# Batch 1's loads and attention pulled into the first layer, global rows on the ACT queue, one score run per pair, in a fused windowed-attention and two-layer kernel

## Chip, cores, metric

One core of one Trainium2 chip. The metric is the device time of one execution in microseconds (us), taken as the median of several executions. Engines are named as in the profile: PE (matmul), PEld (weight load), DVE, ACT, POOL, SP. The granted clock is the share of the full PE clock that the profile shows as granted; a slow PE clock is called cold, a full one warm.

## The reference

Per batch and head there are 512 local rows with a window of 32 to each side, and 32 global rows that see everything and are seen by everything. The attention output (8 batches x 544 rows x 512 columns) goes through two layers with a hard-swish between them.

```python
s_g   = scale * q_g @ concat(k_g, k_l).T;  out_g = softmax(s_g) @ concat(v_g, v_l)
s_ll  = where(|i - j| <= 32, scale * q_l @ k_l.T, -1e9)
out_l = softmax(concat(scale * q_l @ k_g.T, s_ll)) @ concat(v_g, v_l)
x = concat(out_g, out_l).transpose(0, 2, 1, 3).reshape(8 * 544, 512)
h = x @ w_in                       # 512 -> 2048
out = (h * clip(h + 3, 0, 6) / 6) @ w_out   # 2048 -> 512
```

## The kernel before

Attention works on "pairs" (two heads of one batch, `p = 4*b + m`, 32 of them). Layers work on "units": `u1(c)` is one of 16 units of layer 1 (four 512-column matmuls into one PSUM bank, a ReLU on ACT, an eviction `gt` on DVE), `u2(t, c4)` one of 16 units of layer 2 (four matmuls). `M(n)` emits the next n units of the batch before, between pieces of attention. There are seven general PSUM banks. `pin` fixes the order of the instructions traced so far to the program's order; what is not pinned, the build's scheduler may move. Each engine has its own list of instructions; in the trace of the kernel after, all 502 counted instructions of DVE start in the order in which the compiled program lists them (compared by source line).

A pair needs: casts of k, q, v (DVE or POOL), transposes (`emit_T` on PE, `emit_TD` by DMA for batches from 2 on), scores (`emit_S`, two chunks), exponentials on ACT, masks on DVE, `emit_AV`, and for the global rows `emit_SG` and `emit_PG`. `emit_G` casts and transposes the global keys or queries of several batches. `kglob` and `vglob` copy global rows beside a batch's local ones.

```python
# loads, all on SP, through 13 staging tiles
for i in range(NC):  load_w("in", i)
for i in range(NC):
    load_w("out", i)
    if i == 3:
        load_g(1, 4, "kg"); load_g(0, 4, "qg")      # 7 global-row loads, 64 KB each
for p in range(NM, 2 * NM + 1):                     # batch 1 and the next pair
    load(p)
...
# after the attention of batch 0: layer 1 of batch 0 with nothing between its units
for c in range(HEAD, NC):
    u1(c)
for i in range(NC):
    cast_w("out", i, nc.gpsimd)
emit_G(1, 4, "kg"); emit_G(0, 4, "qg")
fill_v(1, nc.vector); fill_vg(1, nc.gpsimd)
kglob(1, nc.gpsimd); vglob(1, nc.gpsimd)
for p in range(NM, 2 * NM):
    cast(p, "k", nc.vector); cast(p, "qv", nc.gpsimd); vshift(p, nc.gpsimd)
M(3)                                                # layer 2 of batch 0 begins
pin(*ALL)
emit_T(4)                                           # attention of batch 1
...
# the loop, one pair a turn; n = how many layer units go where
M(n[0]); emit_S(p + 1, 0)
M(n[1]); emit_S(p + 1, 1); emit_SG(p + 1)
M(n[2]); emit_AV(p); emit_PG(p)
M(n[3]); emit_X(p)
```

The softmax here doesn't subtract the row's maximum and nothing guards it: scores larger than these inputs give would overflow.

Of the kernel before, what the change touches and what calls it, by code (L numbers as in the profile page):

```python
# [14 lines left out]
def kernel(  # L15
# [94 lines left out]
    def stage():  # L110
        return wrk.tile([P, 512], FP32, tag="stg", name="stg", bufs=NSTG)

    def load(p, what="kqv"):
        b, m = divmod(p, NM)
        s = st.setdefault(p, {})
        for c in what:
            src = {"k": k_l, "q": q_l, "v": v_l}[c]
            t = stage()
            if c != "v" and b < NRUN:
                nc.sync.dma_start(out=t.rearrange("p (h x) -> p h x", h=2),  # L120
                                  in_=src[b, 2 * m:2 * m + 2].rearrange("h (p j) d -> p h (j d)", j=NT))
            else:
                nc.sync.dma_start(out=t.rearrange("p (h kb d) -> p (h kb) d", h=2, kb=NT),
                                  in_=src[b, 2 * m:2 * m + 2].rearrange("h (kb p) d -> p (h kb) d", p=P))
            s[c + "f"] = t.rearrange("p (h kb d) -> p kb h d", h=2, kb=NT)
# [12 lines left out]
    def vshift(p, eng, n=1):  # L138
        b, m = divmod(p, NM)
        hs = slice(2 * m, 2 * m + 2 * n)  # L140
        eng.tensor_copy(out=vbs[b % NV][0:D, :, hs, 0:D], in_=vts[b % NV][D:P, :, hs, 0:D])  # L141
# [12 lines left out]
    def load_w(kind, i):  # L154
        t = stage()
        if kind == "in":
            qd, m = divmod(i, NM)
            nc.sync.dma_start(out=t, in_=moe_w_in[m * P:(m + 1) * P, qd * 512:(qd + 1) * 512])
        else:
            nc.sync.dma_start(out=t, in_=moe_w_out[i * P:(i + 1) * P, :])  # L160
        w_st[kind, i] = t

    def cast_w(kind, i, eng):
        if kind == "in":
            qd, m = divmod(i, NM)
            o = w_in_t[m][:, qd * 512:(qd + 1) * 512]
        else:
            o = w_out_t[i // 4][:, i % 4]
        eng.tensor_copy(out=o, in_=w_st[kind, i])

    gst = {}

    def load_g(b0, b1, nm):
        src = {"kg": k_g, "qg": q_g}[nm]
        t = stage()
        for b in range(b0, b1):
            i = b - b0
            nc.sync.dma_start(out=t[i * Sg:(i + 1) * Sg].rearrange("s (h d) -> s h d", h=H),
                              in_=src[b].rearrange("h s d -> s h d"))
        gst[b0, nm] = t  # L180

# [53 lines left out]
    def wrap_q(p):  # L235
        qT = st[p]["qT"]
        nc.gpsimd.tensor_copy(out=qT[:, 0:W], in_=qT[:, Sl:Sl + W])  # L237

    def emit_S(p, ch, pe_mask=False):
        s = st[p]  # L240
        qT, kT = s["qT"], s["kT"]
        if ch == 0:
            s["E"] = wrk.tile([P, 2, 2, Sl], FP16, tag="E", name="E", bufs=3)
        E = s["E"]
        pss = [ps_tile(f"psS{e}") for e in range(2)]
        if pe_mask:
            for e in range(2):
                nc.tensor.matmul(out=pss[e], lhsT=ident, rhs=mneg[:, ch], start=True, stop=False,
                                 skip_group_check=True)
        for w in range(NT):  # L250
            c0 = w * KW if ch == 0 else ((w - 1) % NT) * KW + D
            for e in range(2):
                r = slice(e * D, (e + 1) * D)
                nc.tensor.matmul(out=pss[e][:, w * P:(w + 1) * P], lhsT=kT[r, c0:c0 + P],  # L254
                                 rhs=qT[r, w * P:(w + 1) * P], start=not pe_mask, stop=True,
                                 skip_group_check=True)
        for e in range(2):
            nc.scalar.activation(out=E[:, ch, e], in_=pss[e], func=EXP, scale=qk_scale)  # L258
        for e in range(0 if pe_mask else 2):
            nc.vector.tensor_tensor(out=E[:, ch, e], in0=E[:, ch, e],  # L260
                                    in1=mk[:, ch].rearrange("p w c -> p (w c)"), op=mult)
# [19 lines left out]
    def emit_AV(p):  # L281
        b, m = divmod(p, NM)
        E = st[p]["E"]
        vt, vb = vts[b % NV], vbs[b % NV]
        xn = wrk.tile([P, NT, P], FP16, tag="xn", name="xn", bufs=3)
        st[p]["xn"] = xn
        for w2 in range(NT // 2):
            po = ps_tile("pav").rearrange("p (w c) -> p w c", w=2)
            for i in range(2):
                w = 2 * w2 + i  # L290
                for e in range(2):
                    h = 2 * m + e
                    o = po[:, i, e * DV:e * DV + D + 1]
                    nc.tensor.matmul(out=o, lhsT=E[:, 0, e, w * P:(w + 1) * P],  # L294
                                     rhs=vt[:, w, h, 0:D + 1], start=True, stop=False,
                                     skip_group_check=True)
                    nc.tensor.matmul(out=o, lhsT=E[:, 1, e, w * P:(w + 1) * P],  # L297
                                     rhs=vb[:, (w - 1) % NT, h, 0:D + 1], start=False, stop=True,
                                     skip_group_check=True)
            pv = po[:, :, 0:2 * DV].rearrange("p w (e c) -> p w e c", e=2)  # L300
            rc = wrk.tile([P, 2, 2, 1], FP32, tag="rc", name="rc", bufs=4)
            nc.vector.reciprocal(out=rc, in_=pv[:, :, :, D:D + 1])  # L302
            nc.vector.tensor_tensor(  # L303
                out=xn[:, 2 * w2:2 * w2 + 2].rearrange("p w (e d) -> p w e d", e=2),
                in0=pv[:, :, :, 0:D], in1=rc.to_broadcast([P, 2, 2, D]), op=mult)
# [103 lines left out]
        load(p, "kqv")  # L409
    for i in range(NC):  # L410
        load_w("in", i)
    for i in range(NC):
        load_w("out", i)
        if i == 3:
            load_g(1, 4, "kg")
            load_g(0, 4, "qg")
    for p in range(NM, 2 * NM + 1):
        load(p)

    make_identity(nc, ident)  # L420
    load_vg(0)
# [16 lines left out]
    def fill_v(i, eng):  # L438
        eng.memset(vbs[i], 0.0)
        eng.memset(vbs[i][0:P - W, :, :, D:D + 1], 1.0)  # L440
        eng.memset(vts[i][:, :, :, D:D + 1], 1.0)
# [6 lines left out]
    def fill_vg(i, eng):  # L448
        eng.memset(vgs[i], 0.0)
        eng.memset(vgs[i][rg, :, D:P], 1.0)  # L450
# [38 lines left out]
    emit_S(3, 0, True)  # L489
    emit_X(1)  # L490
    emit_S(3, 1, True)
    emit_AV(2)
    HEAD = 3
    for c in range(HEAD):
# [10 lines left out]
    for t in Egs:  # L505
        nc.vector.memset(t[:, NT], 0.0)
    nc.vector.tensor_scalar(out=mk.rearrange("p c w q -> p c (w q)"), in0=mneg, scalar1=-1.0,
                            scalar2=1.0, op0=is_ge, op1=mult)
    for c in range(HEAD, NC):
        u1(c)  # L510
    for i in range(NC):
        cast_w("out", i, nc.gpsimd)
    emit_G(1, 4, "kg")
    emit_G(0, 4, "qg")
    fill_v(1, nc.vector)
    fill_vg(1, nc.gpsimd)
    kglob(1, nc.gpsimd)
    vglob(1, nc.gpsimd)
    for p in range(NM, 2 * NM):
        cast(p, "k", nc.vector)  # L520
        cast(p, "qv", nc.gpsimd)
        vshift(p, nc.gpsimd)
    M(3)
    pin(*ALL)
    emit_T(4)
    emit_SG(0)
    emit_SG(1)
    M(1)
    emit_SG(2)
    emit_SG(3)  # L530
    emit_S(4, 0)
    M(1)
    for p in range(NM):
        emit_PG(p)
    emit_T(5)
    emit_S(4, 1)
    ones_v(1)
    emit_SG(4)
    emit_XG(0)
    for b in range(2, B):  # L540
        load_vg(b)

    for p in range(NM, NPAIR):
        b, m = divmod(p, NM)
        if p + 5 < NPAIR:
            load(p + 5)
        if 2 * NM <= p + 2 < NPAIR:
            wrap_q(p + 2)
        if p + 4 < NPAIR:
            if m == 0:  # L550
                vglob(b + 1, nc.gpsimd)
            cast(p + 4, "kqv", nc.gpsimd)
            vshift(p + 4, nc.gpsimd)
        if m == 1 and b + 1 < B:
            kglob(b + 1, nc.gpsimd)
        if p == 5:
            load_g(4, B, "kg")
            load_g(4, B, "qg")
        if p == 10:
            emit_G(4, B, "kg")  # L560
            emit_G(4, B, "qg")
        n = (1, 1, 0, 0) if b == 1 else (1, 2, 2, 3)
        if 2 * NM <= p + 3 < NPAIR:
            emit_TD(p + 3)
        if p + 2 < 2 * NM:
            emit_T(p + 2)
        M(n[0])
        if p + 1 < NPAIR:
            emit_S(p + 1, 0)
        M(n[1])  # L570
        if p + 1 < NPAIR:
            emit_S(p + 1, 1)
            emit_SG(p + 1)
        M(n[2])
        emit_AV(p)
        emit_PG(p)
        M(n[3])
        emit_X(p)
        if m == NM - 1:
            emit_XG(b)  # L580
            units += moe_units(lambda mm, b=b: xts[b][mm], Sl, local_dests(b))
        pin(*QUEUES)
    M(len(units))
    units += moe_units(
        lambda mm: xg[:, mm].rearrange("p b s -> p (b s)"), B * Sg,
# [33 lines left out]
```

## Time and profile before

| | before |
|---|---|
| median time | 339.18 us (3 runs, 339.06 to 340.31) |
| span of the profiled run | 337.4 us |
| PE busy | 93% |
| mean granted clock | 0.967 |
| layer 1 of batch 1 starts (chain) | 83.28 us |

The table by windows of the kernel before follows. After the stretch and its length come the busy time of each engine with its instruction count, the granted TensorE clock, the DMA share and GB/s.

```profile
core 0: us, PE busy (x) PEld busy (x) DVE busy (x) ACT busy (x) POOL busy (x), PEclk, DMA share, GB/s
0.00:20.00 20.00, 12.60 (x154) 6.82 (x156) 13.79 (x40) 14.78 (x26) 15.38 (x33) 1.00 0.99 280
20.00:36.80 16.80, 16.08 (x112) 7.80 (x108) 13.57 (x32) 10.60 (x17) 10.47 (x17) 1.00 0.96 294
36.80:83.30 46.50, 36.76 (x412) 20.62 (x412) 30.58 (x73) 22.15 (x54) 35.79 (x59) 0.78 1.12 230
83.30:299.00 215.70, 215.70 (x1925) 107.75 (x1924) 148.26 (x323) 136.81 (x272) 70.98 (x132) 1.00 0.71 140
...
```

From 83.3 to 299 us PE never stands still and its clock is full, so only fewer PE cycles can help there. Between 36.8 and 83.3 us PE stands for 9.7 us, and its clock averages 0.78. The waits of PE in that part (engine, line, what it waited for, then us in total, times, longest):

```profile
PE psTq L213 <- POOL qn L136: 2.6, 1, 2.6
PE psS L254 <- DVE qT L221: 2.3, 2, 2.0
PE psGT L188 <- DVE kgn L185: 1.8, 1, 1.8
PE pg L317 <- ACT Eg L272: 1.5, 1, 1.5
PE psGT L188 <- DVE qgn L185: 1.0, 1, 1.0
...
```

POOL's time line (start, us, engine, line, operation, output and input, count) just before that cast:

```profile
45.77 2.28 POOL L145 COPY vb<-vg 32x512 f16<-32x512 f16 x4
47.99 0.81 POOL L147 COPY vgs<-vg 32x512 f16<-32x512 f16 x1
48.87 0.61 POOL L136 CAST qn<-stg 128x512 f16<-128x512 f32 x1
```

By the landing events packed with the trace, the query that this cast reads had landed at 44.60 us. POOL came to it only after its own w_out casts, fills and global-row copies.

The chain of work that ended last (start, us, what) shows what the scores cost PE in steady state:

```profile
124.85 1.83 PE psH L360 x8
126.68 0.33 PE psS L254 x8
127.01 0.25 PE psSG L271 x5
127.26 1.73 PE psH L360 x8
...
```

Eight layer matmuls take 1.73 us, but 1.83 us right after a score run. A score run of eight matmuls takes 0.33 us.

### The profile page before, as it was taken

How to read it: one execution, taken by the hardware profiler on the slowest of the kernel's cores; microseconds unless marked ns; L12 is line 12 of the kernel's file. 1: busy time of each engine (PE TensorE's matmuls, PEld its weight loads, DVE VectorE, ACT ScalarE, POOL GpSimd, SP SyncE). 2: the span in 40 equal slices, each digit the busy share in tenths (PEclk: the TensorE clock that was granted, in tenths of full speed). 3: DMA queues.
4: the chain of work that ended last, by engine and by line, in shares of the span. 5: the costliest groups of instructions: out<-in, count | busy, mean ns of one | idle time of the engine just before them, and what ended most of it. 6: DMA issues, size and time to landing. Idle time of an engine off the chain costs nothing.

```text
span 337.4 us, 7429 instructions
## 1 busy us (share of the span) xinstructions
PE 314.6 (93%) x2780; PEld 161.0 (48%) x2780; DVE 220.8 (65%) x494; ACT 198.2 (59%) x393; POOL 132.6 (39%) x240
## 2 busy tenths in 40 slices
PE   1989669959999999999999999999999999999994
PEld 0554236535454445454444554454445445444571
DVE  4868846875895588547866787468744882483160
ACT  8648308655883488447844785468645971382260
POOL 5985799863753362319313725182230000000000
PEclk9999876987999999999999999999999999999999
DMA  8999999979995977788799897897943002101202
GB/s 210 318 377 226 338 292 246 175 176 183 198 202 113 213 165 139 151 185 179 140 145 199 174 143 140 176 216 142 137 114 96 18 16 80 62 0 33 84 11 62
DMA packets 139747, 52.92 MB, mean 157 GB/s; under 512 B 127168, under 2 KB 131264, under 8 KB 139712
## 3 DMA queue, kind: packets, MB, share of 16 engines
q1 hardware_dynamic: 137536, 52.19, 71.5%
q0 software_dynamic: 2176, 0.26, 1.2%
q8 instruction: 22, 0.36, 0.5%
q14 instruction: 13, 0.11, 0.1%
HBM read 35.13 MB, written 8.91 MB: 131 GB/s over the span
## 4 chain that ended last, share of the span: by engine, by line
PE 83%; DMA 7%; ACT 3%; DVE 3%; POOL 1%; issue 1%; SPq 1%; DVEq 0%; POOLq 0%
PE po L376 36%; PE psH L360 31%; PE psS L254 5%; DMA stg<-in_moe_w_out_dram 3%; DMA stg<-in_moe_w_in_dram 3%; PE psSG L271 2%; PE pav L297 2%; PE pav L294 2%; PE pg L317 2%; ACT vt L445 1%; DVE E L260 1%; PE psX L333 1%; POOL vb L145 1%; SPq L160 1%; ACT E L258 1%
## 5 line engine op out<-in xcount | busy, mean ns | idle before, releaser
L376 PE MATMUL po<-wout,gt 128*128 128x512 f16 x544 | 131.6, 390 | 0.0
L360 PE MATMUL psH<-xt,win 128*128 128x512 f16 x512 | 117.3, 379 | 0.5 <-DVE xt L337 0.5
L367 DVE SCALAR_TENSOR_TENSOR gt<-t,psH 128x512 f16<-128x512 f32 (+1 forms) x144 | 90.6, 654 | 23.2 <-ACT t L365 21.5
L365 ACT ACTIVATE t<-psH,half_col 128x512 f32<-128x512 f32 (+1 forms) x144 | 92.1, 664 | 21.9 <-PE psH L360 19.1
L258 ACT ACTIVATE E<-psS 128x512 f16<-128x512 f32 x128 | 69.1, 598 | 52.3 <-PE psS L254 52.2
L360 PEld LDWEIGHTS <-win 128*128 128x128 f16 x576 | 53.5, 98 | 53.9 <-issue 0.6
L376 PEld LDWEIGHTS <-gt 128*128 128x128 f16 x544 | 50.9, 100 | 55.9 <-issue 5.4
L260 DVE TENSOR_TENSOR E<-E,mk 128x512 f16<-128x512 f16 x112 | 55.5, 515 | 33.1 <-ACT E L258 32.1
L237 POOL COPY qT<-qT 128x32 f16<-128x32 f16 x24 | 5.0, 209 | 109.9 <-DMA qT<-qn 103.3
L380 ACT COPY ot<-po 128x512 f32<-128x512 f32 x17 | 10.0, 586 | 38.5 <-PE po L376 38.5
L254 PEld LDWEIGHTS <-kT 64*128 64x128 f16 x512 | 15.1, 96 | 28.9 <-issue 25.4
L254 PE MATMUL psS<-qT,kT 64*128 64x128 f16 x512 | 26.2, 225 | 2.3 <-DVE qT L221 2.3
L303 DVE TENSOR_TENSOR xn<-pav,rc 128x256 f16<-128x256 f32 x64 | 26.5, 423 | 1.4
L380 DVE COPY ot<-po 128x512 f32<-128x512 f32 x17 | 11.8, 692 | 21.3 <-PE po L376 21.3
L141 POOL COPY vb<-vt 64x512 f16<-64x512 f16 x32 | 20.7, 647 | 2.1
L136 POOL CAST vt<-stg 128x512 f16<-128x512 f32 x32 | 20.7, 648 | 1.9 <-DMA stg<-in_v_l_dram 1.9
L136 POOL CAST qn<-stg 128x512 f16<-128x512 f32 x32 | 20.2, 630 | 1.6 <-DMA stg<-in_q_l_dram 1.3
L297 PE MATMUL pav<-vb,E 128*128 128x65 f16 x256 | 20.3, 195 | 0.0
L294 PE MATMUL pav<-vt,E 128*128 128x65 f16 x256 | 20.3, 194 | 0.0
L294 PEld LDWEIGHTS <-E 128*128 128x128 f16 x256 | 18.0, 99 | 3.1
L302 DVE RECIPROCAL rc<-pav 128x4 f32<-128x4 f32 x64 | 10.6, 174 | 12.4 <-PE pav L297 12.4
L297 PEld LDWEIGHTS <-E 128*128 128x128 f16 x256 | 17.2, 98 | 2.8
(73 smaller groups left out, 239.6 us busy)
## 6 DMA issues: line engine op xcount, KB each, us to landing
stg<-in_k_l_dram SPq DMA_DIRECT2D x32, 256.0 KB, 3.5
stg<-in_q_l_dram SPq DMA_DIRECT2D x32, 256.0 KB, 4.1
stg<-in_v_l_dram SPq DMA_DIRECT2D x32, 256.0 KB, 4.5
out_dram<-ot SPq DMA_DIRECT2D x24, 256.0 KB, 2.3
stg<-in_moe_w_in_dram SPq DMA_DIRECT2D x16, 256.0 KB, 5.9
stg<-in_moe_w_out_dram SPq DMA_DIRECT2D x16, 256.0 KB, 5.2
out_dram<-ot SPq DMA_DIRECT2D x8, 192.0 KB, 2.2
out_dram<-ot SPq DMA_DIRECT2D x16, 64.0 KB, 1.9
```

The costliest lines, as they stand in the source:

```text
L136: eng.tensor_copy(out=o, in_=s[c + "f"])
L254: nc.tensor.matmul(out=pss[e][:, w * P:(w + 1) * P], lhsT=kT[r, c0:c0 + P], rhs=qT[r, w * P:(w + 1) * P], start=not pe_mask, stop=True, sk ...
L258: nc.scalar.activation(out=E[:, ch, e], in_=pss[e], func=EXP, scale=qk_scale)
L260: nc.vector.tensor_tensor(out=E[:, ch, e], in0=E[:, ch, e], in1=mk[:, ch].rearrange("p w c -> p (w c)"), op=mult)
L294: nc.tensor.matmul(out=o, lhsT=E[:, 0, e, w * P:(w + 1) * P], rhs=vt[:, w, h, 0:D + 1], start=True, stop=False, skip_group_check=True)
L297: nc.tensor.matmul(out=o, lhsT=E[:, 1, e, w * P:(w + 1) * P], rhs=vb[:, (w - 1) % NT, h, 0:D + 1], start=False, stop=True, skip_group_chec ...
L303: nc.vector.tensor_tensor(out=xn[:, 2 * w2:2 * w2 + 2].rearrange("p w (e d) -> p w e d", e=2), in0=pv[:, :, :, 0:D], in1=rc.to_broadcast([ ...
L360: nc.tensor.matmul(out=ps[:, 0:n], lhsT=w_in_t[m][:, c * P:(c + 1) * P], rhs=rhs(m), start=(m == 0), stop=(m == NM - 1), skip_group_check= ...
L365: nc.scalar.activation(out=t1[:, 0:n], in_=ps[:, 0:n], func=RELU, bias=half_col, scale=1.0 / 6.0)
L367: nc.vector.scalar_tensor_tensor(out=gts[c][:, 0:n], in0=t1[:, 0:n], scalar=1.0, in1=ps[:, 0:n], op0=amin, op1=mult)
L376: nc.tensor.matmul(out=po[t][:, 0:dm], lhsT=gts[c][:, t * P:(t + 1) * P], rhs=w_out_t[c // 4][:, c % 4], start=(c == 0), stop=(c == NC - 1))
L380: (nc.scalar.copy if t % 2 else nc.vector.tensor_copy)(out=ot, in_=po[t][:, 0:dm])
```

## The change

The intent: batch 1's data arrive before w_out, so that its attention can fill layer 1 of batch 0 instead of standing in its own stretch; the small global-row loads leave SP's queue; and both score chunks of a pair run together, which needs four PSUM banks at once.

```diff
-        t = stage()
+        t = wrk.tile([P, dm], FP32, tag="ot", name="stg_g", bufs=4) if act else stage()
-            nc.sync.dma_start(out=t[...], in_=src[b]...)
+            (nc.scalar if act else nc.sync).dma_start(out=t[...], in_=src[b]...)
+    def emit_S2(p):             # both chunks' matmuls, then the 4 exponentials and 4 masks
+    for p in range(NM, 2 * NM):
+        load(p, "kqv")
     for i in range(NC):
         load_w("out", i)
-        if i == 3: load_g(1, 4, "kg"); load_g(0, 4, "qg")
-    for p in range(NM, 2 * NM + 1): load(p)
+    load(2 * NM)
     emit_S(3, 1, True)
+    load_g(1, 4, "kg", True)
+    load_g(0, 4, "qg", True)
+    ones_v(1)                   # was unpinned, after the pinned part
     emit_AV(2)
     ...
-    for c in range(HEAD, NC): u1(c)
+    fill_v(1, nc.vector); fill_vg(1, nc.vector)
+    for p in range(NM, 2 * NM): cast(p, "qv", nc.gpsimd); vshift(p, nc.gpsimd)
     for i in range(NC): cast_w("out", i, nc.gpsimd)
+    for c in range(HEAD, HEAD + 4): u1(c)
     emit_G(1, 4, "kg")
+    u1(HEAD + 4)
     emit_G(0, 4, "qg")
-    (fills, global copies on POOL, casts, M(3), pin)
+    u1(HEAD + 5)
+    kglob(1, nc.vector); vglob(1, nc.vector)
+    cast(4, "k", nc.vector)
     emit_T(4)
+    M(1)                        # layer-1 units 9 to 15 from here on
     ...
+    cast(5, "k", nc.vector); emit_T(5)
     ...
-            emit_S(p + 1, 0)
+            emit_S2(p + 1)
         M(n[1])
-            emit_S(p + 1, 1)
```

(Cut: other unit counts per turn in batch 1, key casts of pairs 6 and 7 inside the loop, PE pinned in batch 1's turns, the later global-value loads one batch at a time.)

More of the change, by code (lines that the diff above doesn't have):

```diff
@@ L171, with load_g @@
     gst = {}
-    def load_g(b0, b1, nm):
+    def load_g(b0, b1, nm, act=False):
         src = {"kg": k_g, "qg": q_g}[nm]
-        t = stage()
+        t = wrk.tile([P, dm], FP32, tag="ot", name="stg_g", bufs=4) if act else stage()
         for b in range(b0, b1):
             i = b - b0
-            nc.sync.dma_start(out=t[i * Sg:(i + 1) * Sg].rearrange("s (h d) -> s h d", h=H),
+            (nc.scalar if act else nc.sync).dma_start(out=t[i * Sg:(i + 1) * Sg].rearrange("s (h d) -> s h d", h=H),
                               in_=src[b].rearrange("h s d -> s h d"))
@@ L237, in wrap_q @@
         nc.gpsimd.tensor_copy(out=qT[:, 0:W], in_=qT[:, Sl:Sl + W])
+    def emit_S2(p):
+        s = st[p]
+        qT, kT = s["qT"], s["kT"]
+        E = s["E"] = wrk.tile([P, 2, 2, Sl], FP16, tag="E", name="E", bufs=3)
+        pss = [ps_tile(f"psS{i}") for i in range(4)]
+        for ch in range(2):
+            for w in range(NT):
+                c0 = w * KW if ch == 0 else ((w - 1) % NT) * KW + D
+                for e in range(2):
+                    r = slice(e * D, (e + 1) * D)
+                    nc.tensor.matmul(out=pss[2 * ch + e][:, w * P:(w + 1) * P],
+                                     lhsT=kT[r, c0:c0 + P], rhs=qT[r, w * P:(w + 1) * P])
+        for ch in range(2):
+            for e in range(2):
+                nc.scalar.activation(out=E[:, ch, e], in_=pss[2 * ch + e], func=EXP,
+                                     scale=qk_scale)
+            for e in range(2):
+                nc.vector.tensor_tensor(out=E[:, ch, e], in0=E[:, ch, e],
+                                        in1=mk[:, ch].rearrange("p w c -> p (w c)"), op=mult)
     def emit_S(p, ch, pe_mask=False):
@@ L411 @@
         load_w("in", i)
+    for p in range(NM, 2 * NM):
+        load(p, "kqv")
     for i in range(NC):
         load_w("out", i)
-        if i == 3:
-            load_g(1, 4, "kg")
-            load_g(0, 4, "qg")
-    for p in range(NM, 2 * NM + 1):
-        load(p)
+    load(2 * NM)
     make_identity(nc, ident)
@@ L508 @@
                             scalar2=1.0, op0=is_ge, op1=mult)
-    for c in range(HEAD, NC):
-        u1(c)
+    fill_v(1, nc.vector)
+    fill_vg(1, nc.vector)
+    for p in range(NM, 2 * NM):
+        cast(p, "qv", nc.gpsimd)
+        vshift(p, nc.gpsimd)
+    load_vg(2)
     for i in range(NC):
         cast_w("out", i, nc.gpsimd)
+    for c in range(HEAD, HEAD + 4):
+        u1(c)
     emit_G(1, 4, "kg")
+    u1(HEAD + 4)
     emit_G(0, 4, "qg")
-    fill_v(1, nc.vector)
-    fill_vg(1, nc.gpsimd)
-    kglob(1, nc.gpsimd)
-    vglob(1, nc.gpsimd)
-    for p in range(NM, 2 * NM):
-        cast(p, "k", nc.vector)
-        cast(p, "qv", nc.gpsimd)
-        vshift(p, nc.gpsimd)
-    M(3)
-    pin(*ALL)
+    u1(HEAD + 5)
+    kglob(1, nc.vector)
+    vglob(1, nc.vector)
+    units[:0] = [lambda c=c: u1(c) for c in range(HEAD + 6, NC)]
+    cast(4, "k", nc.vector)
     emit_T(4)
+    M(1)
     emit_SG(0)
@@ L528 @@
     M(1)
+    emit_S(4, 0)
+    cast(5, "k", nc.vector)
+    emit_T(5)
+    M(1)
+    emit_S(4, 1)
     emit_SG(2)
     emit_SG(3)
-    emit_S(4, 0)
     M(1)
@@ L534 @@
         emit_PG(p)
-    emit_T(5)
-    emit_S(4, 1)
-    ones_v(1)
     emit_SG(4)
     emit_XG(0)
-    for b in range(2, B):
-        load_vg(b)
+    pin(*ALL)
     for p in range(NM, NPAIR):
@@ L561 @@
             emit_G(4, B, "qg")
-        n = (1, 1, 0, 0) if b == 1 else (1, 2, 2, 3)
+        n = {4: (1, 1, 1, 0), 5: (1, 1, 1, 0), 6: (1, 1, 1, 2), 7: (2, 2, 2, 2)}.get(p, (1, 2, 2, 3))
+        if m == 2 and b + 2 < B:
+            load_vg(b + 2)
+        if p + 2 < 2 * NM:
+            cast(p + 2, "k", nc.vector)
         if 2 * NM <= p + 3 < NPAIR:
@@ L581 @@
             units += moe_units(lambda mm, b=b: xts[b][mm], Sl, local_dests(b))
-        pin(*QUEUES)
+        pin(*QUEUES, *((ET.PE,) if b == 1 else ()))
     M(len(units))
```

## The prediction

> **What bounds the kernel now.** The table by windows: from 83.3 to 299 us PE is busy 215.7 of 215.7 us at granted clock 1.00: PE-bound. From 36.8 to 83.3 us (layer 2 of batch 0, attention of batch 1) it is busy 36.8 of 46.5 us at clock 0.78. PE's waits there: key/query casts that wait for late batch-1 loads (4.2 + 2.6 us), global-row casts (2.8), a query wrap (2.0), AV/PG (2). Cold matmuls cost too: by the chain, 12 layer-2 matmuls took 5.13 us, warm 12 take 2.60. Estimate for 24.6 to 83.3 us from warm pieces of the chain (a 512-column matmul 0.216 us): 39 us of PE work. So at most 19.5 us, 5.8%, is recoverable; the intended gain lies there.
>
> **Steady state.** In the chain, an 8-matmul score run costs 0.33 us and the next matmuls 0.10 us more (8 layer matmuls take 1.83 us after scores, else 1.73). Where before ran 16 score matmuls together (70.3 us), they took 0.56 us. One run per pair instead of two saves (0.66 - 0.56) + 0.10 = 0.2 us. The Trainium skill, "TensorEngine Tiling (Array Packing)", Key Properties, says that changing tiling mode drains the engine; the 0.10 us agrees. 23 pairs after 83.3 us: -4.8 us. It needs four PSUM banks of seven at once and four exponentials (0.55 us each) in a row. ACT and DVE are 80 to 99% busy in layer-1 stretches, so I let 1 us be lost to waits.
>
> **Head and middle.**
> - The second set of ones (2.13 us on ACT at 5.05 us) moves; the first query copy waited for it (7.08 us): -0.5 us, since casts on POOL hold the rest.
> - Global rows issue from ACT: 7 issues at about 0.5 us (SP's durations), then the ones copies. First ReLU goes from 25.2 to about 27 us.
> - DVE, in program order here, gets batch-1 fills (about 2.4 us) ahead of layer-1 evictions, after the 2.4 us already there (27.9 to 30.2). So evictions 3 to 6 end about 36 us. PE, having filled seven banks by about 28.5 us, stands at the global-key transpose until about 36, gets cold, and later waits for the global-row copies (2.8 us, moved from POOL to DVE) before batch 1's first transposes, about 47 us. By then before had done 7 more layer-1 units (6 us) and 16 layer-2 matmuls (3.5 us).
> - In return the waits on loads go: batch-1 data land by about 38 us, w_out under layer-1 work. w_out loads wait for staging tiles freed by DVE's key casts, so 1 to 2 us of wait may return at layer 2.
> - Sum: layer 1 of batch 1 starts about 84 us instead of 83.3 (+1, range -6 to +4).
>
> **Prediction.** 339.2 + 1 - 0.5 - 4.8 + 1 = 335.9; as waits may be shorter than this in-order addition says, 335.5 us, range 329.5 to 340.5. Faster by over 2%: 0.22; within 2%: 0.76; slower: 0.02.
>
> **What would show it.** Right: PE idle about 28 to 36 us, waiting for DVE's global-key cast, clock 0.5 after it; no PE wait on batch-1 loads; period of a batch after 90 us about 34.4 instead of 35.3 us, PE still 100% busy; batch 1's layer 1 starting at 80 to 87 us. Wrong: PE over 95% busy from 25 to 83 us (then about 325 us); or PE waits on score banks (then no gain of the merged run).
>
> **What would make it wrong.** Another order on DVE or ACT than the program's; DMA issue on ACT far from 0.5 us; a w_out shortage; bank waits.

## The result

The kernel got slower: 352.28 us median (350.96 to 352.80, 4 runs) against 339.63 us (4 runs), ratio 1.0366, 95% interval 1.0328 to 1.0403. Ratios are the mean time of one kernel's fast runs over that of the other's of the same rounds, so they are not quite the ratios of the medians quoted. Executions over 1.5% slower than the fastest of the same kernel are left out of the means.

| | before | after |
|---|---|---|
| span of the profiled run | 337.4 us | 350.3 us |
| mean granted clock | 0.967 | 0.950 |
| first ReLU of layer 1 on ACT | 25.20 us | 31.43 us |
| first transposes of batch 1 on PE | 46.51 us | 53.70 us |
| layer 1 of batch 1 starts | 83.28 us | 99.29 us |
| from there to the last layer's start | 207.65 us | 204.50 us |

The last two rows hold the whole result. The head and middle lost 16.0 us, the steady state gained 3.15 us, and 16.0 - 3.15 is the 12.9 us by which the span grew. (The last layer starts at 290.93 us before and at 303.79 us after. The last row is not quite like for like: after, it holds 368 score matmuls against 352, one pair more, about 0.8 us of work.)

The windows of the kernel after, in the same columns:

```profile
24.20:53.70 29.50, 8.78 (x35) 3.37 (x35) 15.58 (x34) 7.57 (x13) 19.55 (x34) 0.63 1.07 294
53.70:99.30 45.60, 38.08 (x410) 21.56 (x411) 27.36 (x65) 24.45 (x57) 15.81 (x29) 0.87 0.64 126
99.30:303.80 204.50, 204.28 (x1908) 106.49 (x1907) 145.73 (x317) 132.65 (x265) 74.05 (x135) 1.00 0.76 145
...
```

For 29.5 us PE was busy only 8.8 us. From the end of batch 0's attention to batch 1's layer 1 PE stood 9.7 us before (of 58.3, from 24.8 to 83.1 us) and 28.2 us after (of 75.1, the first two rows), while its busy time was 48.6 and 46.9 us. So the whole loss is time in which PE stood; the clock was low in both (0.84 and 0.81 before, 0.63 and 0.87 after). Its waits from 20 to 99.3 us:

```profile
PE psGT L188 <- DVE kgn L185: 13.7, 1, 13.7
PE psTk L213 <- DVE kn L136: 7.8, 3, 4.9
PE psX L353 <- DVE xn L323: 3.6, 3, 3.2
PE psGT L188 <- DVE qgn L185: 2.1, 1, 2.1
...
```

None of them is for a load. PE waits for small work on DVE: casts, and 3.6 us for the normalized attention output (`xn`). Why the casts were late is read from the time lines. First ACT's, with ACTq its queue (start, us, engine, line, operation, output and input, count, and in brackets the idle time before with what ended it):

```profile
20.23 0.59 ACT L278 ACTIVATE E<-psS 128x512 f16<-128x512 f32 x1
20.68 2.46 ACTq L178 DMA_DIRECT2D stg_g<-in_k_g_dram  x2
24.46 4.87 ACTq L178 DMA_DIRECT2D stg_g<-in_q_g_dram  x4
29.38 2.15 ACT L463 COPY vt<-ones 128x504 f16<-128x504 f16 x4 [8.56 <-DMA stg_g<-in_q_g_dram]
31.43 4.14 ACT L385 ACTIVATE t<-psH,half_col 128x512 f32<-128x512 f32 x7
...
```

ACT did nothing for 8.56 us. Each of the seven issues takes a median of 0.32 us by itself (the view of that tile), but they lie up to 29.0 us, because each waits for something first. The compiled program says for what: for a counter of the loads, one of eight that SP's loads use too. The first four of the seven:

```
L178 DMACopy stg_g<-in_k_g_dram 32x8x64 [waits DMAHW0_49]
L178 DMACopy stg_g<-in_k_g_dram 32x8x64 [waits DMAHW3_49]
L178 DMACopy stg_g<-in_k_g_dram 32x8x64 [waits DMAHW6_49]
L178 DMACopy stg_g<-in_q_g_dram 32x8x64 [waits DMAHW1_49]
...
```

So an issue on ACT waits until the earlier load on the same counter has landed. The counter events packed with the trace agree: the first issue (19.77 us) found its counter ready, and each of the other six starts 0.02 us after its counter is complete (20.68 after 20.66, 22.82 after 22.80, up to 29.02 after 29.00). For four of them that earlier load is a 256 KB load of w_in, which takes 5.9 us from issue to landing by the page; for the last two it is one of ACT's own global-row loads. These waits stand in the compiled program, so they could have been read before any run. The Trainium skill, "DMA: Bandwidth & Descriptors", Anatomy of one DMA, says, in a section on DMAs issued from POOL, that a semaphore wait of a DMA takes place on the issuing sequencer before dispatch; this trace agrees for DMAs issued from ACT, and here the sequencer was that of the engine which had to run the ReLUs. (Before, the first ReLU came at 25.20 us.)

Then DVE's line:

```profile
32.14 1.88 DVE L387 SCALAR_TENSOR_TENSOR gt<-t,psH 128x512 f16<-128x512 f32 x3 [7.96 <-ACT t L385]
34.08 0.48 DVE L467 MEMSET vgs<- 128x512 uint32 x1
...
36.38 0.94 DVE L457 MEMSET vb<- 128x1056 uint32 x1 [0.17 <-issue]
...
38.92 2.48 DVE L387 SCALAR_TENSOR_TENSOR gt<-t,psH 128x512 f16<-128x512 f32 x4
41.31 0.84 DVE L185 CAST kgn<-stg_g 96x512 f16<-96x512 f32 x1
```

DVE stood idle for 7.96 us, did three evictions, then 4.8 us of set-up and fills that the program puts there, then four evictions, and only then the cast on which PE stood. And PE's:

```profile
24.23 4.26 PE L380 MATMUL psH<-xt,win 128*128 128x512 f16 x19 [0.52 <-DVE xt L357]
42.21 0.50 PE L188 MATMUL psGT<-ident,kgn 96*128 96x96 f16 x4 [13.72 <-DVE kgn L185]
42.51 1.91 PE L380 MATMUL psH<-xt,win 128*128 128x512 f16 x4
46.48 0.61 PE L188 MATMUL psGT<-ident,qgn 128*128 128x128 f16 x4 [2.06 <-DVE qgn L185]
46.88 1.91 PE L380 MATMUL psH<-xt,win 128*128 128x512 f16 x4
53.70 0.61 PE L213 MATMUL psTk<-ident,kn 128*128 128x128 f16 x4 [4.91 <-DVE kn L136]
...
```

This is a lock-step: one layer unit, a wait for DVE, one transpose, one unit, a wait for DVE. Four matmuls now take 1.91 us here: the granted clock is 0.50 in every 5 us window from 35 to 55 us. The Trainium skill, "TensorE: Matmul & The Clock Gate", What's actually happening, says that the array falls to half clock after an idle window of about 3.4 us; the trace agrees: PE stood from 28.49 us, and the granted clock went to 0.50 at 31.71 us, 3.2 us later.

In the steady state the merged run behaves as meant. The chain of the kernel after:

```profile
143.38 0.55 PE psS L249 x16
143.94 1.83 PE psH L380 x8
145.77 0.15 PE psSG L291 x5
145.92 1.73 PE psH L380 x8
...
```

Sixteen score matmuls take 0.55 us instead of 2 x 0.33, and only one follower pays the 0.10 us (before, a layer run and the global score run both paid, 0.25 us against 0.15 us).

### The profile page after: what moved, and what is told of

The parts are those of the page before. It is cut to its first block, busy times and chain, and to the rows that moved or that the text cites. A ratio compares the mean times of both kernels' runs of the same rounds, so it can differ in the third digit from the quotient of the medians.

```text
span 350.3 us, 7444 instructions
## 1 busy us (share of the span) xinstructions
PE 309.9 (88%) x2780; PEld 162.5 (46%) x2780; DVE 225.4 (64%) x502; ACT 198.8 (57%) x393; POOL 127.9 (37%) x232
## 4 chain that ended last, share of the span: by engine, by line
PE 76%; DVE 8%; DMA 7%; ACT 3%; SPq 2%; issue 1%; POOL 1%; POOLq 0%; DVEq 0%; ACTq 0%
PE po L396 34%; PE psH L380 30%; PE psS L249 4%; DMA stg<-in_moe_w_in_dram 3%; DVE E L256 3%; DVE gt L387 2%; DMA stg<-in_v_l_dram 2%; PE pav L317 2%; PE pav L314 2%; PE pg L337 2%; SPq L120 2%; PE psSG L291 1%; DMA stg<-in_moe_w_out_dram 1%; ACT t L385 1%; DMA stg_g<-in_q_g_dram 1%
## 5 line engine op out<-in xcount | busy, mean ns | idle before, releaser
L396 PE MATMUL po<-wout,gt 128*128 128x512 f16 x544 | 126.8, 381 | 0.0
L380 PE MATMUL psH<-xt,win 128*128 128x512 f16 x512 | 124.1, 389 | 0.8 <-DVE xt L357 0.5
L396 PEld LDWEIGHTS <-gt 128*128 128x128 f16 x544 | 50.1, 98 | 55.0 <-issue 0.6
L256 DVE TENSOR_TENSOR E<-E,mk 128x512 f16<-128x512 f16 x108 | 56.6, 556 | 28.0 <-ACT E L253 25.9
L253 ACT ACTIVATE E<-psS 128x512 f16<-128x512 f32 x108 | 55.6, 603 | 17.0 <-PE psS L249 17.0
L249 PEld LDWEIGHTS <-kT 64*128 64x128 f16 x432 | 12.4, 95 | 13.0 <-issue 9.9
L249 PE MATMUL psS<-qT,kT 64*128 64x128 f16 x432 | 17.0, 219 | 0.9 <-DVE qT L221 0.9
L136 POOL CAST kn<-stg 128x512 f16<-128x512 f32 x27 | 17.1, 634 | 0.6
```

The costliest lines, as they stand in the source:

```text
L136: eng.tensor_copy(out=o, in_=s[c + "f"])
L249: nc.tensor.matmul(out=pss[2 * ch + e][:, w * P:(w + 1) * P], lhsT=kT[r, c0:c0 + P], rhs=qT[r, w * P:(w + 1) * P])
L253: nc.scalar.activation(out=E[:, ch, e], in_=pss[2 * ch + e], func=EXP, scale=qk_scale)
L256: nc.vector.tensor_tensor(out=E[:, ch, e], in0=E[:, ch, e], in1=mk[:, ch].rearrange("p w c -> p (w c)"), op=mult)
L380: nc.tensor.matmul(out=ps[:, 0:n], lhsT=w_in_t[m][:, c * P:(c + 1) * P], rhs=rhs(m), start=(m == 0), stop=(m == NM - 1), skip_group_check= ...
L396: nc.tensor.matmul(out=po[t][:, 0:dm], lhsT=gts[c][:, t * P:(t + 1) * P], rhs=w_out_t[c // 4][:, c % 4], start=(c == 0), stop=(c == NC - 1))
```

## Experiments

Three theories were on the table. Theory 1: the loss comes from the order on in-order engines (ACT behind DMA issues, DVE's fills ahead of evictions, casts right before the transposes that need them), and the load order itself is good. Theory 2: loading batch 1 ahead of w_out starves something. Theory 3: the merged score runs wait for PSUM banks. Times come from different chips, so I compare ratios to the kernel before.

| run | median us | ratio to before (95%) | expected us |
|---|---|---|---|
| the change | 352.28 | 1.0366 (1.0328 to 1.0403) | 335.5 |
| e1_g_on_sp | 348.33 (fast runs) | 1.0239 (1.0200 to 1.0278) | 346 |
| e2_fills_early | 348.56 | 1.0255 (1.0208 to 1.0302) | 348 |
| e3_both | 345.96 | 1.0173 (1.0140 to 1.0207) | 344 |
| e4_before_merged | 334.66 | 0.9847 (0.9821 to 0.9873) | 335.5 |
| e5_k_on_pool | 337.52 (fast runs) | 0.9925 (0.9878 to 0.9973) | 340 |
| e6_ahead | 332.58 | 0.9790 (0.9762 to 0.9819) | 324 |
| e7_wout_first | 337.76 | 0.9953 (0.9927 to 0.9979) | 332 |
| e8_spread | 330.24 | 0.9721 (0.9676 to 0.9766) | 326.5 |

All were correct against the reference. By the 2% rule e1 and e2 are slower, e8 faster, e4, e5 and e7 the same, e3 and e6 unclear; where an interval leaves out 1, the difference is still clear of noise.

### e1_g_on_sp: global rows issued by SP

```diff
-            (nc.scalar if act else nc.sync).dma_start(...)
+            nc.sync.dma_start(...)
+    load_g(1, 4, "kg", True); load_g(0, 4, "qg", True)   # after w_in, ahead of batch 1
     for p in range(NM, 2 * NM):
         load(p, "kqv")
```

> The changed kernel, with the seven global-row loads issued by SP between w_in and batch 1 instead of by ACT; all else stays. Theory 1 (in-order queues: ACT stood 8.6 us behind these issues, then DVE's fills delayed the layer-1 evictions, then PE stood 13.7 us at the global-key transpose): first ReLU from 31.4 to about 24.6 us, the key cast on DVE from 41.3 to about 35 us, PE's long wait from 13.7 to about 7 us, time 352.3 - 6.5 = about 346 us (343 to 348). Theory 2 (batch 1's loads ahead of w_out starve the queue): the loads come later still by the 0.45 MB of global rows, so 352 us or more. Theory 3 (merged score runs wait for PSUM banks): unchanged, 352 us.

Measured: 348.33 us, the median of the three fast runs (347.01, 348.61, 348.33; 348.47 with the slow one), ratio 1.0239 against 1.0366. The gain of about 4 us (1.27% of 340) answers Theory 1 in sign and kind, but is smaller than the 6.5 us that I expected, and the time lies just outside my range. Putting 0.45 MB more ahead of batch 1's loads did not cost time on balance, which speaks against Theory 2, though only weakly; e7_wout_first tests it.

### e2_fills_early: DVE's fills into its idle time

```diff
+    (set-up of batch 0's global values, mask, fill_v(1), fill_vg(1))   # moved up
     for c in range(HEAD):
         u1(c, range(3, 4))
-    (the same)
```

> The changed kernel, with DVE's fills, mask and global-value copy (about 4.8 us) moved ahead of the first three evictions, into the stretch from 24.2 to 32.1 us where DVE was idle; global rows still on ACT. Theory 1: first ReLU stays at 31.4 us, evictions 3 to 6 end 4.8 us sooner, key cast at about 37 us instead of 41.3, time about 348 us (345 to 350). Theories 2 and 3: unchanged, 352 us.

Measured: 348.56 us, ratio 1.0255, a gain of about 4 us. The first ReLU stayed (31.32 us), the global-key cast came at 36.22 us instead of 41.31, and PE's long wait fell from 13.7 to 7.9 us. This is what Theory 1 said, within 0.8 us.

### e3_both

> Both edits. Theory 1: the fills now run while ACT writes ones and the first ReLUs, so they overlap only in part: key cast at about 33.5 us, PE's long wait about 5.5 us, time about 344 us (341 to 347), not the sum of both gains. Theories 2 and 3: 352 us or more.

Measured: 345.96 us, ratio 1.0173. First ReLU at 25.71 us, key cast at 34.39 us, PE's long wait 5.8 us. Batch 1's first transposes come at 46.76 us instead of 53.70, where the prediction had put them (47). The two gains don't add up (about 4 + 4, together 6.6 us), because fills and ReLUs now share the same stretch. Theories 2 and 3 give nothing here. But 6.6 us are not the whole loss. What is left in PE's waits from 20 to 95 us:

```profile
PE psTk L213 <- DVE kn L136: 10.1, 3, 4.7
PE psGT L188 <- DVE kgn L185: 5.8, 1, 5.8
PE psGT L188 <- DVE qgn L185: 2.2, 1, 2.2
...
```

### e4_before_merged: only the merged runs, in the kernel before

```diff
-            emit_S(p + 1, 0)
+            emit_S2(p + 1)
         M(n[1])
-            emit_S(p + 1, 1)
```

> The kernel before with only the merged score runs in the loop. If a merged run saves 0.2 us of tile-mode switches and bank waits cost about 1 us in all, about 335.5 us (334 to 337.5), period of a batch about 34.1 us instead of 35.0, PE still busy 100% after 90 us. Theory 3 (bank waits eat it): 339 us or more, with PE idle time put down to ACT or DVE in layer-1 stretches.

Measured: 334.66 us (334.44 to 334.87), ratio 0.9847. In the trace PE has no wait at all from 83 to 330 us, and layer 1 of batch 1 starts at 83.25 us as before (83.28): the whole gain, 4.6 us of span, lies after it. Theory 3 falls. Those are 22 pairs (352 score matmuls), 0.21 us each. This one part of the change was worth 1.5% by itself (interval 1.3 to 1.8%); the change as a whole lost it again, and more.

### e5_k_on_pool: batch 1's key casts as the data land

Edit on top of e3_both:

```diff
     for p in range(NM, 2 * NM):
-        cast(p, "qv", nc.gpsimd)
+        cast(p, "kqv", nc.gpsimd)
-    cast(4, "k", nc.vector)
-    cast(5, "k", nc.vector)
-        if p + 2 < 2 * NM:
-            cast(p + 2, "k", nc.vector)
```

> The run with both edits, with batch 1's key casts moved from DVE to POOL, which then casts each pair's keys as they land. In the run with both edits PE waited 14.2 us in four places for DVE key casts that stand behind evictions and global-row copies in DVE's order. Theory 1: those four waits fall to a few us (the first pair's score matmuls still wait for the key copy behind the global-row copies), w_out's loads no longer wait for DVE's casts, time 346 - 6 = about 340 us (336 to 343). Theory 2 (batch 1's early loads starve w_out): 346 us, with PE waits moved to w_out.

Measured: 337.52 us, the median of three fast runs (335.36 to 338.50; a fourth, at 341.44, was slow), ratio 0.9925, a gain of 2.5% or about 8.4 us on e3_both. (My expectation counted 14.2 us in four places. One of the four, 4.1 us, is PE's wait at the very start of the kernel; the three in question sum to 10.1 us.) The waits on key casts are gone from the window of 20 to 90 us:

```profile
PE psGT L188 <- DVE kgn L185: 5.8, 1, 5.8
PE psX L353 <- DVE xn L323: 4.0, 4, 3.3
...
```

With this one edit more the kernel is faster than before, if only by 0.75%. The edit changes the engine and the place of the cast at once; PE waits for w_out in neither run, so staging tiles that come free sooner for w_out are not the gain. It is the largest single item: in e3_both the four pairs' keys landed at 30.4, 33.4, 36.1 and 38.8 us, and DVE cast them at 46.3, 53.7, 62.2 and 65.2 us. Of the 8.7 us by which batch 1's layer 1 starts earlier, 4.9 come ahead of batch 1's first transposes (41.88 us instead of 46.76) and 3.8 behind them.

### e6_ahead: every operand made one or two units ahead

On top of e3_both, the stretch was rewritten with the same load order and the same idea of attention inside layer 1:

```diff
+    fill_v(1, nc.gpsimd); fill_vg(1, nc.gpsimd)
+    for p in range(NM, 2 * NM): cast(p, "kqv", nc.gpsimd); vshift(p, nc.gpsimd)
     for c in range(3, 7): u1(c)
+    cast_G(1, 4, "kg")          # the cast alone, one unit ahead
+    u1(7)
+    cast_G(0, 4, "qg")
+    u1(8); emit_G(1, 4, "kg")   # transposes
+    u1(9); emit_G(0, 4, "qg"); kglob(1, nc.vector)
+    u1(10); emit_T(4)
+    u1(11); emit_SG(0); emit_SG(1); emit_T(5)
+    u1(12); emit_S(4, 0); u1(13); emit_S(4, 1); emit_SG(2); emit_SG(3)
+    u1(14); (global-value copies of batch 1 on ACT); emit_PG(0..3); emit_SG(4)
+    u1(15); emit_XG(0)
```

> The same load order, merged score runs and attention of batch 1 inside layer 1, but every cast stands one or two layer-1 units ahead of the transpose that needs it; batch 1's fills and key casts on POOL, global-value copies on ACT, global rows on SP. Theory 1: no PE wait over 3 us from 25 us on, batch 1's layer 1 starts at 69 to 74 us instead of 99.3, time about 324 us (320 to 330). Theory 2: w_out is late, PE waits 8 us or more for it, time 335 us or more.

Measured: 332.58 us, ratio 0.9790. Layer 1 of batch 1 starts at 79.7 us instead of 99.3, and from 25 us on no wait of PE is over 2.3 us and none is for w_out. Theory 1 is right about what to do, and its number is wrong: about 324 us was expected, and 332.58 is outside my range. Some of the reasons are in the trace, and e8_spread takes them up. One was new to me. DVE's mask op, and POOL beside it:

```profile
27.50 2.64 DVE L535 TENSOR_SCALAR mk<-mneg 128x1024 f16<-128x1024 f16 x1
30.06 4.25 DVE L396 SCALAR_TENSOR_TENSOR gt<-t,psH 128x512 f16<-128x512 f32 x7
```

```profile
27.45 0.62 POOL L169 CAST win<-stg 128x512 f16<-128x512 f32 x1 [0.38 <-DMA stg<-in_moe_w_in_dram]
28.00 1.86 POOL L468 MEMSET vb<- 128x2112 f16 x1
29.92 0.40 POOL L469 MEMSET vb<- 96x32 f16 x1
```

The mask op took 0.43 us in the kernel before and 2.64 us here. It started 0.05 us after a POOL cast had started and ended at 30.14 us, 0.28 us after POOL's long fill. In e7_wout_first, which has the same ops here, it started at 27.1 us, ahead of the fill at 27.95 us, and took 0.46 us. The Trainium skill, "SBUF — State Buffer", Who interferes with whom, says that such a DVE copy-like op and a POOL op can exclude each other from a shared port pair for a whole instruction. The trace fits that; no run here measures it alone.

### e7_wout_first: the same with w_out ahead again

```diff
-    for p in range(NM, 2 * NM): load(p, "kqv")
     for i in range(NC): load_w("out", i)
+    for p in range(NM, 2 * NM): load(p, "kqv")
     (and POOL's casts in the same order)
```

> The previous run with w_out's loads and casts put back ahead of batch 1's. Theory 1: batch 1's first keys land at about 40 us instead of 31, PE waits about 7 us at the first transposes and 1 to 3 us at later pairs, time about 8 us above the previous run, about 332 us (328 to 337). Theory 2: the same or faster than the previous run.

Measured: 337.76 us, ratio 0.9953, 5.2 us slower than e6_ahead on the same chip. I had expected 8 us, on a base that was itself too low, so the time lies just outside my range. The largest wait from 25 to 85 us is now

```profile
PE psTk L222 <- POOL kn L136: 8.6, 1, 8.6
```

which is the first key of batch 1, late behind w_out: it landed at 42.17 us, and POOL was done with its w_out casts at 42.10 us. The run turned both round, the loads and POOL's casts, and does not tell them apart. So the order of the change, loads and casts together, is good by 5 us where the work that uses the early data can run. Theory 2 falls.

### e8_spread: three more waits taken away

On top of e6_ahead: batch 1's value tile zeroed by ACT at about 8 us and its global tile by POOL at about 5 us; the global-value copies on ACT moved next to the ones copies at about 23 us; mask and batch 0's global set-up later on DVE; the second global rows loaded right after w_out.

```diff
     emit_T(0)
+    nc.scalar.memzero(vbs[1])
...
     ones_v(1)
+    (global-value copies of batch 1, nc.scalar.copy)
...
-    fill_v(1, nc.gpsimd); fill_vg(1, nc.gpsimd)
-        if p == 5: load_g(4, B, "kg"); load_g(4, B, "qg")
+    load_g(4, B, "kg", True); load_g(4, B, "qg", True)    # after w_out
```

> The run with casts ahead, with three waits of its trace taken away: (1) batch 1's fills leave POOL's stretch at 28 us, where DVE's mask op took 2.64 us beside a POOL fill instead of 0.43 us (now zeroed by ACT at about 8 us and by POOL at about 5 us; mask and global-value set-up of batch 0 stand later on DVE); (2) the global-value copies on ACT move from 45.8 us, where exponentials waited behind them, to about 23 us, where ACT is idle; (3) the second global rows are loaded right after w_out, so that the hoisted cast on DVE doesn't wait for them ahead of the last query wrap (2.3 us of PE wait). Theory 1: mask op back at about 0.45 us, first layer-1 eviction from 30.1 to about 26 us, PE waits between 28 and 52 us from about 8 to about 3 us and the wait at the last query wrap gone, time 332.6 - 6 = about 326.5 us (323 to 330). If PE is by now held by something else (w_out, or the attention chain itself), 331 us or more.

Measured: 330.24 us (329.40 to 331.69), ratio 0.9721, faster than the kernel before by 2.8%; the next best, e6_ahead, has an interval that just touches this one's. Against e4_before_merged (0.9847), all the rest of the change, so mended, is worth 1.3%. The mask op is back at 0.42 us. Expected were 323 to 330 us, so it just misses. What holds PE from 25 to 85 us has changed in kind:

```profile
PE psS L258 <- POOL qT L246: 2.7, 2, 2.5
PE po L405 <- POOL wout L169: 2.4, 5, 0.8
PE psS L258 <- DVE qT L230: 1.4, 1, 1.4
...
```

PE now waits for w_out and for the first pair that comes through a DMA transpose, that is for data, no longer mainly for the order of casts. Layer 1 of batch 1 starts at 77.3 us.

## Why the prediction was wrong

Predicted were 335.5 us with a range of 329.5 to 340.5; measured were 352.28 us.

- **The steady state: right.** "-4.8 us", of which I "let 1 us be lost to waits", became 4.6 us in e4_before_merged, with no loss to waits. PE stayed 100% busy, and the matmuls after a score run take 0.10 us more, as read beforehand. The Trainium skill, "TensorEngine Tiling (Array Packing)", Key Properties, states the drain, and the traces agree. In the change itself the gain was 3.15 us, or about 4 us with the one pair more that this stretch holds.
- **The head: right.** The step from batch 0's attention to the last quarter of the first layer units moved from 24.79 to 24.23 us (predicted -0.5 us).
- **The mechanism of the first wait: right, its size wrong.** PE did stand at the global-key transpose, behind DVE's fills, and then ran cold. But the step "Global rows issue from ACT: 7 issues at about 0.5 us (SP's durations), then the ones copies. First ReLU goes from 25.2 to about 27 us" failed. I priced an issue by its own duration. What counted was the wait ahead of each issue: ACT stood 8.56 us, and the first ReLU came at 31.43 us. The cast on which PE stood came at 41.31 us, not at 36. e1_g_on_sp and e2_fills_early each gave back about 4 us, both together 6.6 us, and with both batch 1's first transposes came at 46.76 us, as predicted.
- **The sum failed:** "Sum: layer 1 of batch 1 starts about 84 us instead of 83.3 (+1, range -6 to +4)". It started at 99.29 us. Of the 15.3 us that are missing, 6.7 lie ahead of batch 1's first transposes (53.70 us instead of 47) and 8.6 behind them (45.6 us instead of the 37 that the sum left). The second part is the larger, and it is a credit that did not exist. Before, PE took 36.8 us from those transposes to batch 1's layer 1; with the 9.5 us of work that the prediction saw moved behind them that makes 46.3, so by these figures the 37 took it that about 9 us of waits would go. Measured were 45.6. In that stretch PE stood 7.5 us: 2.9 for key casts, 3.4 for `xn` (DVE ran masks and evictions first), 0.9 for a query wrap, 0.2 for a copy. I had seen the first lock-step (a PE transpose behind a DVE cast behind the evictions), but not that it comes again for the key casts of each pair: the cast stands right ahead of its transpose in the program, and behind evictions whose matmuls PE has only just run. e5_k_on_pool, which breaks it for the keys alone, gives back 8.4 us, somewhat under half of it behind the first transposes. Even in e8_spread the stretch behind them takes 42.9 us (34.4 to 77.3).
- **"In return the waits on loads go": this step failed, as there were none to go.** I had put 4.2 + 2.6 us of PE's waits in the kernel before down to late batch-1 loads. The 4.2 us are the start of the kernel, up to 4.15 us, where PE waits for the very first load; I had read the list of waits of the whole span without its window. The 2.6 us, for a query cast on POOL, are POOL's order: the query landed at 44.60 us, and POOL, busy with its own w_out casts, fills and global-row copies, cast it at 48.87 us. So most of what PE waited for from 20 to 83.3 us were casts and copies in the order of DVE and POOL, which the change did not take away but put into layer 1. The batch-1 loads did come earlier (first key at 29.7 us instead of 43.4), and e7_wout_first shows that their order, with POOL's casts in the same order, is worth 5.2 us.
- **w_out:** the shortage of 1 to 2 us that I allowed for did not show as a PE wait in the change, as PE was later than w_out. It shows only in e8_spread (2.4 us).

What stays open: how the remaining difference between e5_k_on_pool and e4_before_merged (about 2.7 us) divides between the global-row casts and the cold clock. An estimate of what the cold clock costs in the change: from batch 0's attention to batch 1's layer 1 PE was busy 46.9 us (445 matmuls, clock 0.63 and 0.87) and in e8_spread 43.1 us (450 matmuls, clock 0.97), so about 4 us; the kernel before, with 48.6 us (466 matmuls, clock 0.84 and 0.81), paid no less. The long collision of DVE and POOL was seen in one place of one run; the same mask op took 0.64 us in e2_fills_early and 0.80 in e5_k_on_pool, and the global-key cast 0.84 us in the change but 0.42 in e2_fills_early, which was not taken apart.

## What to carry to other kernels

An instruction put on another engine's queue brings its waits with it: here a DMA issue on a compute engine cost that engine the time until its semaphore was ready, not the 0.3 us of the issue. A wait that ends with a cast is a wait for data only if the data had not landed before; look up the landing. When attention is woven into a stretch of matmuls, place every cast and copy at least one unit ahead of the matmul or transpose that reads it, in the order of its own in-order engine; where it stood directly ahead, the two engines ran in turns and the TensorE clock fell to 0.50 as well. Try the parts of a bundle one by one: here one part was worth 1.5%, another (the load order, with POOL's casts in the same order) was worth about 1.6% once the casts stood ahead, and together, as first written, they lost 3.7%.

## What the Trainium skill lacked or had wrong

- "DMA: Bandwidth & Descriptors", Issuing engines are not separate DMA queues: it says that issuing from several engines only saves sequencer time, which is usually small. It doesn't warn that the issuing compute engine can lose far more than it saves. Here seven 64 KB loads on ACT held it for 8.56 us, with a median of 0.32 us for an issue alone, as six of them waited for a counter that an earlier load, most often one of 256 KB, still held.
- "TensorEngine Tiling (Array Packing)", Key Properties, states the drain at a change of mode without a size. Here leaving the 64-row mode cost 0.10 us, and one run of sixteen 128-column score matmuls took 0.55 us against 2 x 0.33 us in two runs.
- "SBUF — State Buffer", Who interferes with whom: the rule fits, but has no example of a plain POOL fill. Beside a fill of 1.86 us, and started 0.05 us after the start of a POOL cast, a DVE op of 0.43 us took 2.64 us.
- No page that I used has the lock-step of two in-order engines: 10.1 us in three waits of e3_both, for casts of keys that had landed 16 us and more before.
